# A fused attention and two-layer chain: the first 768 tokens as six tiles of four groups of 32 queries, ordered by a plan that models transfers

## The chip, the cores and the metric

One core of a Trainium2 chip runs the kernel. The metric is device time in microseconds (us) of one execution, less is better. The engines have their usual short names: PE is TensorE (matrix products; PEld its weight loads), DVE is VectorE, ACT is ScalarE, POOL is GpSimd, SP is SyncE, which only issues transfers.

## What is computed

The input is q, k, v (batch 4, 8 heads, 576 tokens, 64 wide) and the weights of two layers. The attention has two parts that are added: a coarse one on means over four tokens, and a local one in which each query sees the keys at a distance under 4.

```python
q_d = q.reshape(B, H, Sd, factor, D).mean(axis=3)    # same for k, v
out_up = np.repeat(sm_attn(q_d, k_d, v_d), factor, axis=2)
mask = np.abs(pos[:, None] - pos[None, :]) < factor
out_local = softmax(where(mask, scale * q @ k.T, -1e9)) @ v
x = (out_up + out_local), tokens as rows             # 2304 x 512
h = x @ w_in;  g = s * relu(h) ** 2 + b;  x = g @ w_out       # 2048 wide
out = ((x @ w_a) * (x @ w_b)) @ w_out2                        # 1536 wide
```

All is float32 to the outside. Inside, each large operand is split into a high and a low part, and a product is the sum of three.

## The kernel before

Every piece of work is a task with an engine, an assumed duration, the tasks it needs, the buffers it takes and gives back, and a due time. `Program.order` plays all tasks through once while the program is built, takes the one that can start first (ties: the one due first), and so writes out the order of every engine. The assumed times set that order alone; on the chip each engine runs its list in order and waits on semaphores.

The work comes in phases. The first layer goes over six blocks of 384 tokens (`BLOCKS`), each with 16 steps of the hidden width (`a_iter`: products `h` at L1059 to L1061, ReLU and square on ACT, split on DVE at L1087, products `acc` at L1102 to L1104, two steps later). The second layer goes over three blocks of 768 tokens. Ahead of block 0 and alongside it, the ramp makes what it needs:

- `down` (from L553): the coarse part, for each batch and each of four pairs of heads. DVE or POOL sums q and k over four tokens (L582; L584 and L585), PE makes the scores (L620), DVE and ACT the softmax (L634 to L662), PE transposes and multiplies by the values (L671, L691), ACT copies to `up` (L703). For batch 0 the values are summed by DVE (L603). For later batches `pool_in` loads them and lets six transfers, issued by POOL, add to them in memory (L551).
- `tile_job` (from L729): the local part of 96 tokens (`TQ`), for tokens 0 to 767. The scores of 96 queries against 102 keys (`TW`) for 8 heads are two products with the mask (L774) and eight with q and k (L780). DVE takes maxima (L802), ACT makes eight exponentials with their sums (L816), DVE normalizes (L824 to L831), PE transposes (L839), ACT copies (L849), PE multiplies by the values (L857), DVE adds the coarse part (L871), and `split_x` makes the high and the low part (L497, L501).
- `w_slice` (from L367): each of 32 weight slices of the first layer comes in a 64-bit form; three ACT instructions (L349, L342, L378) and three of DVE (L354, L362, L383) turn it into the two parts.

For tokens from 768 on, `unit` makes the local part on DVE (L908 to L1015), in the time of the blocks before. The buffers of the ramp are named in `RAMP_BUFS`; `keep_warm` fills waits of PE ahead of the first step with products of zeros (L273).

## Time and profile before

| | us |
|---|---|
| median of 3 runs | 933.05 |
| all runs | 932.78, 933.05, 938.63 |
| profiled execution, span from first to last instruction | 932.3 |
| what lies around it, median less span | 0.75 |
| PE busy in the span | 913.2 (98%) |
| DVE busy | 789.9 (85%) |
| ACT busy | 497.4 (53%) |
| first product `h` of block 0 | 59.2 |

The profiled execution has no time of its own in the results beside its span, so the span is set against the median. A busy share is an average over phases: in the first 150 us DVE and ACT are far above theirs. A row of a timeline gives start and length; the lengths overlap by some 0.1 to 0.2 us, so what an instruction costs its engine is the step from its start to the next start.

### The profile page before, as it was taken

To read this page: it belongs to the slowest core of one execution; us is meant where nothing else is said; L and a number is where in the kernel's file an instruction comes from. 1 tells how busy PE (TensorE), PEld (TensorE's weight loads), DVE (VectorE), ACT (ScalarE), POOL (GpSimd) and SP (SyncE) were. 2 spreads that over 40 slices of the span, in tenths; PEclk is the share of its full clock that TensorE was granted. 3 is DMA by queue.
4 is the path that set the end of the run, shared out by engine and by line. 5 is a ranking of instruction groups with operands and counts; after the bars stand their busy time and mean duration, and the time that the engine had idled before them with its cause. 6 is when DMAs were issued, how large, how long until landed. Compare 5 with 4: busy or idle time off the path is not lost.

```text
span 932.3 us, 14367 instructions
## 1 busy us (share of the span) xinstructions
PE 913.2 (98%) x5319; PEld 847.0 (91%) x5319; DVE 789.9 (85%) x1388; ACT 497.4 (53%) x1144; POOL 69.7 (7%) x70
## 2 busy tenths in 40 slices
PE   8988999999999999999999999999999999999997
PEld 4667989998999899999999999999999999999996
DVE  6988998999999999995977999879877778877753
ACT  4989995345445443535988555335433336433322
POOL 2241201021322200000000000000000000000000
PEclk9998999999999999999999999999999999999999
DMA  7869626224354332313477342012200010300001
GB/s 206 241 174 332 156 90 194 82 82 133 115 115 114 103 107 69 102 29 136 148 262 261 122 122 82 23 44 81 102 22 3 24 43 13 102 29 18 1 1 69
DMA packets 46864, 96.76 MB, mean 104 GB/s; under 512 B 6393, under 2 KB 21337, under 8 KB 46409
## 3 DMA queue, kind: packets, MB, share of 16 engines
q1 hardware_dynamic: 39160, 92.77, 31.0%
q0 software_dynamic: 7200, 2.67, 2.5%
q8 instruction: 42, 0.69, 0.3%
q10 hardware_dynamic: 432, 0.39, 0.1%
q14 instruction: 30, 0.24, 0.1%
HBM read 83.22 MB, written 12.58 MB: 103 GB/s over the span
## 4 chain that ended last, share of the span: by engine, by line
PE 84%; DVE 5%; ACT 4%; issue 3%; DMA 2%; POOL 1%; SPq 0%; ACTq 0%
PE ab L1347 28%; PE acc L1102 7%; PE acc L1103 6%; PE h L1059 6%; PE acc L1104 6%; PE h L1061 6%; PE h L1060 6%; PE acc L1488 5%; PE acc L1489 5%; PE acc L1487 5%; DVE pr L969 1%; DMA pv<-in_vd_dram 1%; ACT z L342 1%; DMA tq<-in_bmask_dram 1%; ACT w L378 1%
## 5 line engine op out<-in xcount | busy, mean ns | idle before, releaser
L1347 PE MATMUL ab<-xo,w 128*128 128x384 f32 x1376 | 273.7, 338 | 0.4 <-DVE u L1390 0.4
L1347 PEld LDWEIGHTS ab<-xo,w 128*128 128x128 f32 x1376 | 246.1, 188 | 16.3 <-DVE u L1390 0.7
L1102 PE MATMUL acc<-gh,w 128*128 128x384 f32 (+1 forms) x384 | 134.2, 350 | 4.0 <-ACT w L816 2.0
L1103 PE MATMUL acc<-gl,w 128*128 128x384 f32 x384 | 131.2, 342 | 0.0
L1059 PE MATMUL h<-xsh,w 128*128 128x384 f32 x384 | 131.1, 341 | 0.0
L1104 PE MATMUL acc<-gh,w 128*128 128x384 f32 (+1 forms) x384 | 130.5, 340 | 0.0
L1061 PE MATMUL h<-xsh,w 128*128 128x384 f32 x384 | 129.0, 336 | 0.0
L1060 PE MATMUL h<-xsl,w 128*128 128x384 f32 x384 | 129.0, 336 | 0.0
L1076 ACT ACTIVATE u<-h 128x384 f32<-128x384 f32 x96 | 47.1, 491 | 116.3 <-PE h L1061 114.9
L1463 ACT ACTIVATE gh<-u 128x384 fp32r<-128x384 f32 x69 | 36.2, 524 | 84.6 <-DVE u L1424 50.5
L1102 PEld LDWEIGHTS acc<-gh,w 128*128 128x128 f32 x384 | 73.0, 190 | 8.1 <-ACT w L816 2.6
L1059 PEld LDWEIGHTS h<-xsh,w 128*128 128x128 f32 x384 | 72.2, 188 | 2.4 <-issue 2.0
L1103 PEld LDWEIGHTS acc<-gl,w 128*128 128x128 f32 x384 | 73.1, 190 | 0.9 <-DVE gl L1087 0.9
L1104 PEld LDWEIGHTS acc<-gh,w 128*128 128x128 f32 x384 | 73.0, 190 | 0.0
L1060 PEld LDWEIGHTS h<-xsl,w 128*128 128x128 f32 x384 | 72.2, 188 | 0.0
L1061 PEld LDWEIGHTS h<-xsh,w 128*128 128x128 f32 x384 | 72.1, 188 | 0.0
L1087 DVE TENSOR_TENSOR gl<-u,gh 128x384 fp32r<-128x384 f32 x96 | 54.3, 565 | 15.4 <-ACT gh L1083 15.2
L1371 ACT ACTIVATE w<-ab 128x384 f32<-128x384 f32 x31 | 15.2, 491 | 95.2 <-PE ab L1347 93.4
L1489 PE MATMUL acc<-w,gl 128*128 128x512 f32 x138 | 54.4, 394 | 0.0
L1488 PE MATMUL acc<-w,gh 128*128 128x512 f32 x138 | 54.3, 394 | 0.0
L1487 PE MATMUL acc<-w,gh 128*128 128x512 f32 x138 | 54.2, 393 | 0.0
L354 DVE TENSOR_SCALAR w<-w 128x512 uint16<-128x512 f32 x61 | 45.6, 767 | 8.3 <-ACT w L349 8.0
(207 smaller groups left out, 1743.9 us busy)
## 6 DMA issues: line engine op xcount, KB each, us to landing
w<-in_w_a_dram SPq DMA_DIRECT2D x26, 512.0 KB
w<-in_w_o_dram SPq DMA_DIRECT2D x25, 512.0 KB
bk<-in_ku_dram SPq DMA_DIRECT2D x22, 320.0 KB
bk<-in_vu_dram SPq DMA_DIRECT2D x22, 320.0 KB
w<-wod SPq DMA_DIRECT2D x12, 512.0 KB
w<-in_w_b_dram SPq DMA_DIRECT2D x10, 512.0 KB
x2d<-ev SPq DMA_DIRECT2D x24, 192.0 KB
x<-x2d SPq DMA_DIRECT2D x3, 1536.0 KB
```

The lines of the kernel that those rows point to most:

```text
L1059: nc.tensor.matmul(out=st["h"], lhsT=w[:, 0, k], rhs=hi[:, k], start=(k == 0), stop=False)
L1060: nc.tensor.matmul(out=st["h"], lhsT=w[:, 0, k], rhs=lo[:, k], start=False, stop=False)
L1061: nc.tensor.matmul(out=st["h"], lhsT=w[:, 1, k], rhs=hi[:, k], start=False, stop=(k == HP - 1))
L1076: A_.activation(out=st["u"], in_=st["h"], func=ACTF.Relu)
L1087: V.tensor_tensor(out=st["lo"], in0=st["u"], in1=st["hi"][:, :n].bitcast(F32), op=ALU.subtract)
L1102: nc.tensor.matmul(out=acc, lhsT=wh, rhs=st["hi"], start=(f == 0), stop=False)
L1103: nc.tensor.matmul(out=acc[:, :n], lhsT=wh, rhs=st["lo"], start=False, stop=False)
L1104: nc.tensor.matmul(out=acc, lhsT=wl, rhs=st["hi"], start=False, stop=(f == FA - 1))
L1347: nc.tensor.matmul(out=o, lhsT=w[:, k], rhs=x, start=(not more and k + n == 0), stop=(k == 1 and n == 2), skip_group_check=more,)
L1487: nc.tensor.matmul(out=acc, lhsT=gh, rhs=w[:, 0], start=first, stop=False)
L1488: nc.tensor.matmul(out=acc, lhsT=gh, rhs=w[:, 1], start=False, stop=False)
L1489: nc.tensor.matmul(out=acc, lhsT=gl, rhs=w[:, 0], start=False, stop=last)
```

## The change

Tokens 0 to 767 are worked on in six tiles of 128 tokens, each of four groups of 32 queries that see 38 keys each (`TQ` 32, `TW` 38, `NQ` 4). The groups lie side by side in the partitions (rows 0, 32, 64, 96) of one score bank, so a row of scores has 8 x 38 = 304 columns instead of 8 x 102 = 816. DVE takes the maxima and subtracts them, writing each head into 64 columns, ACT makes one exponential of the whole tile, DVE sums it. Two heads at a time go through one transposition of 128 x 128 and lie at rows 0 and 64; the values are loaded twice for that, by four transfers a tile (32 and 6 rows at rows 0 and 64). One tile (512 to 639) has tokens of two batches. Scores and outputs are 32 products each instead of 8.

Besides: the values of batch 0 are summed by two additions for each pair of heads, from one load into a `w` buffer. The casts of the mask and of the unit matrix go from DVE to POOL, as does a clearing of the exponentials' two buffers. ACT loads the exponential's table by a small instruction at the start. The summed q and k have four buffers each instead of one, the exponentials two of their own. The plan now models transfers: sixteen engines and partition groups (`Wire`, `wires`), a queue of eight, a transfer's start and landing, and POOL's adding transfers one after another; its due times and assumed times of PE are new.

```diff
-TQ = 96
+TQ = 32
-JOBS = ["TTTTTT", "TTUUU", "UUUUu", "uUUUU"]
+NQ = 4
+TT = NQ * TQ
+JOBS = ["G" * 18, "GGGGGGUUU", "UUUUu", "uUUUU"]
...
-T0, STEP = 40.2, 4.018 / 384
-LEAD = 26.6
-DUE_DOWN = (12.1, 7.8, 2.1, 22.5)
-DUE_NEXT = (60.0, 0.0)
-DUE_TILE = (8.3, 20.6, 22.0)
-DUE_JOB = (11.6, 11.7, 14.9)
...
-WARM, FILL_MIN, FILL_MAX = 18, 1, 20
...
-RAMP_BUFS = {"dq": 2, "dk": 2, "dv": 2, "qd": 1, "kd": 1, "vp": 4, "tq": 1, "tk": 1, "tv": 2, "e": 1, "x": 1, "z": 2}
+T0, STEP = 29.1, 4.018 / 384
+LEAD = 28.4
+DUE_DOWN = (12.1, 3.1, 6.3, 19.4)
+DUE_NEXT = (72.9, 0.0)
+DUE_TILE = (9.3, 25, 22.0)
+DUE_JOB = (11.6, 13.1, 12.9)
...
+WARM, FILL_MIN, FILL_MAX = 18, 0, 20
...
+RAMP_BUFS = {"dq": 2, "dk": 2, "qd": 4, "kd": 4, "tq": 1, "tk": 1, "tv": 1, "e": 2, "x": 1, "z": 2}
...
+            for n, parts in enumerate(t.dma):
+                done = wire.send(s + (DMA_START + ISSUE * n if t.eng == "SP" else POOL_START), parts) + DMA_LAND
+                t.end = max(t.end, done)
+                if t.eng == "SP":
+                    landed.append(done)
+                else:
+                    adding = done + POOL_NEXT
...
+def wires(rows, pieces, size, base=0, adds=False):
+
+    n = max(i for i in range(1, 17) if rows % i == 0)
+    per = rows // n
+    took = per * pieces * (0.038 if adds else 0.003 + size / 21.4e3)
+    engines = [(i, took, {(base + i * per) // 8, (base + i * per + per - 1) // 8}) for i in range(n)]
+    ports = {}
+    for r in range(base, base + rows):
+        ports[r // 8] = ports.get(r // 8, 0.0) + pieces * size * (0.2 if adds else 1.0) / 20e3
+    return engines, list(ports.items())
 
...
+
     def consts():
+        n = n_bufs["r"]["e"]
+        add("POOL", 2.0, e_init, acq=[("re",)] * n, rel=["re"] * n, due=-1e6)
...
+        add(name, cost(3 * TW), mc_fn, ["bm"], ["const"], rel=["rtq"], due=DUE_CONST + 5)
 
...
-                    "POOL" if r else "SP", 1.25, fn, (), [("pv", b)] if r == 3 else (), () if r + kh else [("pv",)], (), due,
-                    [t[kh]] if r else [t[0]] if kh else after, seen=6.0,
+                    "POOL" if r else "SP", 1.25 if r else ISSUE, fn, (), [("pv", b)] if r == 3 else (), () if r + kh else [("pv",)], (), due,
+                    [t[kh]] if r else [t[0]] if kh else after, order=kh if r == 0 else 0, seen=0.1, dma=[wires(HK, HP, 512, 0, r > 0)],
...
-            return st["vp", kh] if b == 0 else pooled[b][:, kh, hp]
+            def lv(p):
...
+
...
+            def vprep(p):
+                x = st["v"]
+                eng.tensor_tensor(out=x[:, :, 0:2], in0=x[:, :, 0:2], in1=x[:, :, 2:4], op=ALU.add)
+                eng.tensor_tensor(out=x[:, :, 0], in0=x[:, :, 0], in1=x[:, :, 1], op=ALU.add)
...
+            st["v"] = tv_slot(p[0])
+            for a, r in parts:
+                for u in range(2):
+                    nc.sync.dma_start(
+                        out=st["v"][u * 64 + a:u * 64 + a + r],
+                        in_=tv[j0:j0 + NQ, a:a + r, u * HP * D:(u + 1) * HP * D].rearrange("g k (h d) -> k g h d", d=D),
+                    )
+
+        parts = ((0, 32), (32, TW - 32))
+        t_v = add(
+            "SP", 4 * ISSUE, l_v, (), [("tv", i)], [("rtv", "w")], after=after, seen=0.1,
+            dma=[wires(r, NQ, 1024, u * 64 + a) for a, r in parts for u in range(2)],
+        )
...
+            sc = st["sc"] = [bank(p[h], [TT, HP, TW], "sc") for h in range(2)]
+            runs = [(0, NQ)] if len(set(variant)) == 1 else [(g, g + 1) for g in range(NQ)]
...
+                for g, e in runs:
+                    nc.tensor.matmul(
+                        out=sc[h][g * TQ:e * TQ], lhsT=identb[:, g:e].rearrange("p g q -> p (g q)"),
+                        rhs=bmaskb[:, variant[g]].unsqueeze(1).to_broadcast([TQ, HP, TW]), start=True, stop=False,
+                    )
...
+                    for g in range(NQ):
+                        q, k, k0, k1 = qk(g, hp)
+                        nc.tensor.matmul(
+                            out=sc[h][g * TQ:g * TQ + TQ, hp, k0:k1], lhsT=q[h * D:h * D + D], rhs=k[h * D:h * D + D],
+                            start=False, stop=(hp == HP - 1),
+                        )
+
...
+            nb = st["nb"] = pools[ph].tile([TT, 2, HP], F32, tag="tnb", name="tnb", bufs=6)
             for h in range(2):
-                V.tensor_reduce(out=nb[:, h * HP:h * HP + HP], in_=st["sc"][h], axis=AX.X, op=ALU.max)
-
-        def m2_fn(p):
-            V.tensor_scalar(out=st["nb"], in0=st["nb"], scalar1=-scale, scalar2=None, op0=ALU.mult)
-
-        chain("DVE", [(2 * dve(HP * TW), m_fn), (0.07, m2_fn)], [("tsc", i)], [("tnb", i)])
+                V.tensor_reduce(out=nb[:, h], in_=st["sc"][h], axis=AX.X, op=ALU.max)
+
+        def d_fn(p):
+            st["w"] = e_slot(ts.picks[2])
+            e = st["w"][:, :NH * 64].rearrange("p (m h u k) -> p h u m k", m=2, h=2, u=2)
+            for h in range(2):
+                V.tensor_tensor(
+                    out=e[:, h, :, :, :TW], in0=st["sc"][h].rearrange("p (u m) k -> p u m k", u=2),
+                    in1=st["nb"][:, h].rearrange("p (u m) -> p u m", u=2).unsqueeze(3).to_broadcast([TT, 2, 2, TW]),
+                    op=ALU.subtract,
+                )
...
+        half = 2 * dve(HP * TW)
+        chain("DVE", [(half, m_fn), (half, d_fn)], [("tsc", i)], [("tnb", i)], [pick(ts, 0), pick(ts, 1)])
...
+            A_.activation(out=e_view(), in_=e_view(), func=ACTF.Exp, scale=scale)
...
+        def n0_fn(p):
+            sm = st["sm"] = pools[ph].tile([TT, NH], F32, tag="tsm", name="tsm", bufs=6)
+            V.tensor_reduce(out=sm, in_=e_view(), axis=AX.X, op=ALU.add)
...
+            e, sm = e_view(), st["sm"]
+            V.tensor_tensor(out=e, in0=e, in1=sm.unsqueeze(2).to_broadcast([TT, NH, TW]), op=ALU.mult)
+
+        chain("DVE", [(dve(NH * TW), n0_fn), (0.07, n1_fn), (0.12, n2_fn), (dve(NH * TW), n3_fn)], [("te", i)], [("ta", i)])
...
-            at = st["at"] = [bank(p[h], [TW, HP, TQ], "at") for h in range(2)]
-            for h in range(2):
-                for hp in range(HP):
-                    nc.tensor.transpose(at[h][:, hp], st["e"][:, h * HP + hp], ident[:TQ, :TQ])
+            at = st["at"] = bank(p[0], [128, HP, TT], "at")
+            for n in range(HP):
+                nc.tensor.transpose(at[:, n], st["w"][:, n * 128:n * 128 + 128], ident)
...
-            aT = st["aT"] = st["w"][:TW, :2 * HP * TQ].rearrange("p (a h q) -> p a h q", a=2, h=HP)
-            for h in range(2):
-                A_.activation(out=aT[:, h], in_=st["at"][h], func=ACTF.Copy)
-
-        add("ACT", 2 * act(HP * TQ, True), c_fn, [("tat", i)], [("taT", i)], rel=[pick(tt, 0), pick(tt, 1)])
+            aT = st["aT"] = st["w"][:, :HP * TT].rearrange("p (a q) -> p a q", a=HP)
+            A_.activation(out=aT[:64 + TW], in_=st["at"][:64 + TW], func=ACTF.Copy)
...
+            o = st["o"] = [bank(p[u], [128, 2, TT], "o") for u in range(2)]
+            for n in range(HP):
+                m, h = divmod(n, 2)
+                for g in range(NQ):
+                    for u in range(2):
+                        nc.tensor.matmul(
+                            out=o[u][h * D:h * D + D, m, g * TQ:g * TQ + TQ], lhsT=st["v"][u * 64:u * 64 + TW, g, n],
+                            rhs=st["aT"][u * 64:u * 64 + TW, n, g * TQ:g * TQ + TQ], start=True, stop=True,
+                        )
```

On DVE, a tile among the first four, before (`tnb`: maxima, `tsm`: sums, `sc`: scores, `vp`: pooled values of batch 0):

```order
L603 TENSOR_REDUCE vp<-dv 72x128 x2
L802 TENSOR_REDUCE tnb<-sc 96x4 x2
L824 TENSOR_SCALAR tsm<-tsm 96x8
L805 TENSOR_SCALAR tnb<-tnb 96x8
L827 RECIPROCAL tsm<-tsm 96x8
L831 TENSOR_TENSOR w<-w,tsm 96x816
```

and now (L732 is of the coarse part):

```order
L732 TENSOR_TENSOR w<-w,sm 72x576
L889 TENSOR_REDUCE tnb<-sc 128x4 x2
L895 TENSOR_TENSOR e<-sc,tnb 128x2x2x38 x2
L911 TENSOR_REDUCE tsm<-e 128x8
L914 TENSOR_SCALAR tsm<-tsm 128x8
L917 RECIPROCAL tsm<-tsm 128x8
L921 TENSOR_TENSOR e<-e,tsm 128x8x38
```

The multiplication of 816 columns becomes one of 304, a subtraction and a sum are new, and the instruction behind the subtraction is the sum, which needs ACT's exponential. The value reductions (L603) are gone.

On POOL, the second batch's preparation (`dk`, `dq` are summed to `kd`, `qd`; the number tells one buffer's use from another's) and the adding transfers (`pv`), before:

```order
L585 TENSOR_TENSOR qd_348<-dq_259 128x144
L551 DMA pv_181<-in_vd_dram 72x4x128 x4
L584 TENSOR_TENSOR dk_343<-dk_343 128x144x2
L585 TENSOR_TENSOR kd_676<-dk_343 128x144
L584 TENSOR_TENSOR dq_377<-dq_377 128x144x2
L585 TENSOR_TENSOR qd_707<-dq_377 128x144
L551 DMA pv_181<-in_vd_dram 72x4x128
L584 TENSOR_TENSOR dk_469<-dk_469 128x144x2
```

and now, from the end of the second pair's preparation on:

```order
L659 TENSOR_TENSOR qd_554<-dq_320 128x144
L625 DMA pv_376<-in_vd_dram 72x4x128
L658 TENSOR_TENSOR dk_548<-dk_548 128x144x2
L659 TENSOR_TENSOR kd_641<-dk_548 128x144
L658 TENSOR_TENSOR dq_550<-dq_550 128x144x2
L659 TENSOR_TENSOR qd_734<-dq_550 128x144
L658 TENSOR_TENSOR dk_618<-dk_618 128x144x2
L659 TENSOR_TENSOR kd_774<-dk_618 128x144
L658 TENSOR_TENSOR dq_630<-dq_630 128x144x2
L659 TENSOR_TENSOR qd_807<-dq_630 128x144
L625 DMA pv_376<-in_vd_dram 72x4x128 x5
L625 DMA pv_1408<-in_vd_dram 72x4x128 x6
```

Before, one add stood ahead of the first preparation, four behind the first pair's and one behind the second pair's. Now one stands behind the second pair's and five behind the last, with the six of the next batch (`pv_1408`) right behind them.

On PE, where the second batch's summed values (`pv`) are first read, before:

```order
L1061 MATMUL h<-xsh,w 128x384
L620 MATMUL sc<-kd,qd 72x144 x4
L671 MATMUL at<-ident,w 72x72 x8
L691 MATMUL o<-w,pv 64x144 x4
L774 LDWEIGHTS identb
L774 MATMUL sc<-bmaskb,identb 96x408
```

and now:

```order
L1197 MATMUL acc_1188<-gh_1303,w_1300 128x386
L1198 MATMUL acc_1188<-gl_1327,w_1300 128x384
L1199 MATMUL acc_1188<-gh_1303,w_1300 128x386
L762 MATMUL o_1361<-w_565,pv_376 64x144 x4
L762 MATMUL o_1369<-w_727,pv_376 64x144 x4
L762 MATMUL o_1378<-w_817,pv_376 64x144 x4
L762 MATMUL o_1389<-w_917,pv_376 64x144 x4
L928 MATMUL at_1402<-ident_75,e_1197 128x128 x4
L1154 MATMUL h_1412<-xsh_119,w_1347 128x384
```

Before, they are read after six `h` products of block 0, for one pair of heads at a time; now all four pairs are read in one piece, after five groups of `h` and four of `acc`.

## Rows read from the trace of the kernel before

**Rows 1.** Busy time by stretch: PE, PEld, DVE, ACT, POOL; granted clock, DMA share, GB/s.
```profile
...
64.40:142.30 77.90, 73.78 (x446) 68.47 (x446) 70.87 (x137) 76.54 (x180) 8.85 (x6) 0.96 0.63 193
147.90:508.80 360.90, 360.48 (x2161) 350.60 (x2161) 326.93 (x483) 194.27 (x435) 39.49 (x38) 1.00 0.41 125
```

**Rows 2.** Single lines over the run: duration min/median/max ns, first and last start.
```profile
...
L1059 PE MATMUL h<-xsh,w x384: 331/336/446, 59.2 to 504.1; 128*128 128x384 f32 x192
...
L383 DVE TENSOR_TENSOR w<-z,w x32: 645/689/744, 51.0 to 142.3; 128x512 fp32r<-128x512 f32 x32
```

**Rows 3.** Timeline of ACT: start, length, instruction (idle before it, releaser).
```profile
...
22.60 0.36 ACT L816 ACTIVATE w<-sc,tnb 96x102 f32<-96x102 f32 x1
22.83 0.22 ACT L816 ACTIVATION_READ_ACCUMULATOR w<-sc,tnb 96x1 f32 x1
...
25.16 0.74 ACT L683 ACTIVATE w<-at 72x288 f32<-72x288 f32 x2
...
30.73 0.87 ACT L849 ACTIVATE w<-at 102x384 f32<-102x384 f32 x2
31.47 0.31 ACT L703 ACTIVATE up<-o 128x144 f32<-128x144 f32 x1
...
60.55 0.68 ACT L349 ACTIVATE w<-w 128x512 int32<-128x512 uint16 x1
61.11 1.25 ACT L342 ACTIVATE z<-w 128x512 f32<-128x512 f32 x2
```

**Rows 4.** Timeline of DVE: a wait at 8 us, and a tile after 32 us.
```profile
...
8.14 0.75 DVE L582 TENSOR_REDUCE kd<-w 128x144 f32<-128x576 f32 x1 [3.10 <-PE sc L620]
...
32.52 1.99 DVE L603 TENSOR_REDUCE vp<-dv 72x128 f32<-72x512 f32 x2
34.42 1.06 DVE L802 TENSOR_REDUCE tnb<-sc 96x4 f32<-96x408 f32 x2
35.40 0.16 DVE L824 TENSOR_SCALAR tsm<-tsm 96x8 f32<-96x8 f32 x1
...
35.83 1.00 DVE L831 TENSOR_TENSOR w<-w,tsm 96x816 f32<-96x816 f32 x1
36.76 1.06 DVE L802 TENSOR_REDUCE tnb<-sc 96x4 f32<-96x408 f32 x2
```

**Rows 5.** Timeline of TensorE: small products of a tile; the end of block 0.
```profile
...
35.59 0.94 PE L780 MATMUL sc<-w 64*96 64x102 f32 x16
...
36.75 0.88 PE L857 MATMUL o<-w,tv 102*64 102x96 f32 x16
...
144.75 0.34 PE L1059 MATMUL h<-xsh,w 128*128 128x384 f32 x1
...
147.90 0.33 PE L1102 MATMUL acc<-gh,w 128*128 128x386 f32 x1
```

**Rows 6.** Timeline of POOL, adding transfers; TensorE, the first product that reads their sum.
```profile
...
42.14 1.19 POOL L551 DMA_DIRECT2D pv<-in_vd_dram  x1 [9.15 <-issue]
...
84.98 1.19 POOL L551 DMA_DIRECT2D pv<-in_vd_dram  x1 [9.81 <-issue]
95.41 1.66 POOL L551 DMA_DIRECT2D pv<-in_vd_dram  x1 [9.24 <-issue]
...
106.25 1.60 POOL L551 DMA_DIRECT2D pv<-in_vd_dram  x1 [3.28 <-issue]
111.39 1.67 POOL L551 DMA_DIRECT2D pv<-in_vd_dram  x1 [3.54 <-issue]
...
61.76 0.71 PE L691 MATMUL o<-w,pv 72*64 72x144 f32 x8
```

**Rows 7.** Timeline of DVE, then of TensorE, at the start of block 2.
```profile
...
216.83 0.68 DVE L501 TENSOR_TENSOR xsl<-x,xsh 128x512 fp32r<-128x512 f32 x1
...
218.23 0.44 PE L1059 MATMUL h<-xsh,w 128*128 128x384 f32 x1
```

More of the change, by code (lines that the diff above doesn't have):

```diff
@@ L84 @@
         "eng", "dur", "fn", "deps", "succ", "acq", "picks", "rel", "due", "lead", "share", "num", "left", "ready", "start",
-        "end", "fill", "seen",
+        "end", "fill", "seen", "dma", "order", "wait",
     )
@@ L278, in fn @@
             nc.sync.dma_start(out=dst, in_=src)
[L280 removed]
+        dma = [wires(rows, pieces, nbytes / rows / pieces, base)]
+        return add("SP", ISSUE, fn, reads, writes, acq, rel, due, after, seen=0.1, dma=dma)
     WIDE = ("att", "h", "acc")
@@ L342, in z_fn @@
             A_.activation(out=st["z"], in_=high, func=ACTF.Copy, scale=2.0 ** -112)
-        tz = add("ACT", 0.56, z_fn, [("st", k)], [("z", k)], acq, after=first)
+        tz = add("ACT", 0.56, z_fn, [("st", k)], [("z", k)], acq, after=first, wait=PATIENCE)
         def a_fn(picks):
```

310 lines of the change are left out of this document (160 added, 150 removed).

## The prediction

> **What bounds the kernel now.** I read the busy time by stretch first [rows 1]. From 147.9 us on, TensorE is busy without a gap (360.48 of 360.90 us) and its work there is untouched by the change. What can move lies before. That ramp has three marks [rows 2]: the first product of block 0 (L1059) at 59.2, the first weight slice finished by DVE (L383) at 51.0, the 32nd and last at 142.3. The last accumulation of block 0 starts at 147.9 [rows 5]; call this mark M. The kernel's end follows M as long as nothing after it runs dry. At TensorE's own pace of 0.175 us a product (18 products from 144.75 to 147.90 [rows 5]) the 384 products ahead of M take 67.2 us; they took 88.7. The reason: between 64.4 and 142.3 ACT is busy 76.54 of 77.90 us and DVE 70.87 [rows 1]. ACT makes the weight slices, three instructions for each, and between them runs the tiles' exponentials. So the ramp is ACT's, with DVE a few us behind it.
>
> **Change part by part.** I price by the step from one instruction's start to the next one's.
>
> ACT: eight exponentials of a tile run from 22.60 to 25.16, 2.56 us, and its two copies from 30.73 to 31.47, 0.74 [rows 3]. Eight tiles: 26.4 us go. What comes are six exponentials of 304 columns and six copies of 512. Neither shape is in the trace: bounds are 0.23 (a 102-column exponential, 22.60 to its read at 22.83) and 0.56 (512 columns, 60.55 to 61.11) [rows 3]; I take 0.35 and 0.50, 5.1 us. ACT saves 21 us (20 to 24). The table load is moved to where ACT is idle anyway.
>
> DVE: two maxima over 408 columns take 0.98 (34.42 to 35.40), the three small steps 0.43, the multiplication over 816 columns 0.93, a value reduction 0.95 [rows 4]. Eight tiles and eight reductions: 18.7 + 7.6 = 26.3 us, and 0.5 for the two casts that go to POOL. 408 and 816 columns give 1.1 ns a column and 0.05 fixed. So a new tile costs two maxima and two subtractions of 152 columns (0.21 each), a sum and a multiplication of 304 (0.38 each) and two small steps (0.27): 1.9 us, six times 11.3; the value sums become four pairs of additions, 512 and 256 columns, 0.60 + 0.33, 3.7. The adding of the coarse half and the split have as many elements as before. DVE saves about 12 us (9 to 14, if the new shapes cost nothing more or each costs a third more).
>
> The head, up to the first slice on DVE at 51.0: in DVE's order the old head holds six tiles' maxima and multiplications and all eight reductions (21.6 us), the new one four tiles, the additions, and 4.2 us of the second batch's coarse softmax and 1.1 of weight work that now stand ahead: 16.7. Net 4.5 us less, with the smaller steps. The 3.10 us that DVE waited for TensorE at 8.14 [rows 4], because the buffer for the pooled keys was single, goes too: there are four now, and next late is the data itself. Against it, a tile now waits between the subtraction and the sum for ACT's one exponential, with little behind it in DVE's order: I charge 0.65 for each of four. First slice: 51.0 - 4.5 - 3.1 + 2.6 = 46. The first product stands behind the scores of all of batch 1, which need POOL's preparation, but that is earlier in POOL's order now; I put it at 47 (42 to 53) instead of 59.2.
>
> From there to M: TensorE has 67.2 us of products, plus one tile's scores, two tiles' transposes and outputs, and the coarse outputs of batch 1. A tile's score products are 64 records instead of 16, the outputs 64 instead of 16, of 38 and 32 columns instead of 102 and 96. Old: 16 records in 0.94 and 0.88 us [rows 5], 0.055 each. If time goes with columns, an output is 1.2 us; if with records, 3.5. I take 2.0 for either, as the masks come on top 2.5 for the scores. A tile's transposes I take at 0.55, batch 1's coarse outputs at 0.65 each as before (0.71 with its tail [rows 6]): 2.5 + 1.1 + 4.0 + 2.6 = 10.2. That makes 77.4. Summing the new orders from first to last slice, DVE needs 71 us and ACT 73. All three lie within 7 us, so none is bound alone: I add 2.
>
> Trainium skill, "TensorEngine Tiling (Array Packing)", section on instruction overhead: a product of few columns takes as long as one of 60, so a tiling factor should not be taken from a dimension that is already small. By it an output would be an estimated 64 x 0.055 x 60/96 = 2.2 us, which the old rows, all of 96 columns and more, can't confirm; the sum would be 0.5 us longer.
>
> The chained adds: POOL adds batch 1's values in six transfers that each wait for the one before. Before, five of the six go out by 42.14 and TensorE reads them from 61.76 on [rows 6]. Now one goes out ahead of the last preparations and five behind them, and TensorE's order has batch 1's outputs (L762) behind five products and four accumulations, 19 us of work, about 21 us after its first: at 68. The step from add to add was 10.43 (84.98 to 95.41) with weights crowding the queues, 5.14 (106.25 to 111.39) with few [rows 6]. The second add I put at 33, an estimate: two preparations, the first add and two more preparations go ahead of it, and the old fifth went out at 42. With the middle step, 7.8, the last lands at 33 + 5 x 7.8 = 72. TensorE waits 4 us, and behind it wait ACT's copies L774 in its order, with the weight slices, and one SP load of values with them. Part is caught up since ACT and DVE worked ahead: 2.5. Ends: 0 and 18.
>
> Trainium skill, "DMA: Bandwidth & Descriptors", section on the anatomy of one GpSimd DMA: 2.0 us plus bytes over 436 GB/s for each. For 147 KB that is an estimated 2.3 us, and this wait would be nothing. The trace disagrees: no step from add to add is under 5 us, so it stays in.
>
> M = 47 + 77.4 + 2 + 2.5 = 129 against 147.9: 19 us earlier. Behind M nothing changes: same units, same loads. But DVE is just in time there: the split of block 2's last unit starts at 216.83, its first product at 218.23 [rows 7]. So the end moves by the smaller of the two shifts, M's 19 and that of DVE's last slice, 142.3 - (46 + 71 + some 5 of waits) = 20. The profiled execution's span is 932.3, the median of the runs 933.05, 0.75 around it. 932.3 - 19 + 0.75 = 914.
>
> **Rivals.**
> A. As summed: 914, own range 908 to 920.
> B. The adds decide. With 10.4 us a step the last lands at 85, TensorE stands 17 us, and 4 are left: 929. For: the weight loads are let go just then. Against: the short step of 5.14. If POOL starts five later and a step is 12 to 13 us, the last lands at 98 to 103; from 89 on the gain is gone, and at 101 the time is 945, slower. That is the case on the other side.
> C. Small products go by records: a tile's scores and outputs 3.5 us each, on the path of the first three tiles, and 4 us more behind the first product. First product at 52, M at 138: 923. For: half of what the old products did is loading weights. Against: between them TensorE has warm-up products to drop.
> D. Fewer waits than charged: first product at 42, no wait on the adds, 78 to M at 120: 905. For: ACT's 21 us are on the path nearly in full.
> E. The gain doesn't reach the end, since the units behind M run dry: DVE, held behind TensorE's wait for the adds in its own order, finishes its slices only 5 us earlier, and block 2 waits for it [rows 7]: 928. Against: DVE's sum is 12 us smaller.
>
> **Chances.** A 0.52, D 0.17, C 0.13, B in part (921 to 929) 0.06, B slower 0.04, E 0.08. What a measurement of this kernel tells from no change is about 1%, 9.3 us. Faster by more: A, D, nearly all of C and B in part, 0.86. Within 1%: most of E and what is left of C and B, 0.09. Slower: 0.05. The range runs from D's 905, less 1, to the far side of C, 925.
>
> **What would show it.** Right: the first L1154 near 47, the last L457 near 122, the last accumulation of block 0 near 129, and 932.3 less that shift at the end; ACT below 85% in 64 to 120 with DVE above it. The adds are seen in POOL's steps and in TensorE's wait before L762; the small products in L862 and L947, start to start. Wrong: a first product after 53, a wait over 8 us at L762, or an end that moved less than M.

## The result and the profile after

The two kernels were run in turn: before 935.69 us (median of 4 runs, 932.78 to 938.63), changed 923.4 us (median of 4, 919.97 to 927.55). The ratio is 0.988 with a 95% interval of 0.985 to 0.992, so the change makes the kernel 1.2% faster; by the ratio that is 11.1 us of 935.69, by the two medians 12.3. Forecast were 914, 19 us less than the 933.05 of the runs known then, with a range of 904 to 925: the direction and the range held, the gain is some 60% of what was forecast. The profiled execution took 923.98 us, with a span of 922.2, 10.1 below the span of before.

| mark, us | before | forecast | after |
|---|---|---|---|
| first slice done by DVE | 51.0 | 46 | 51.8 |
| first product of block 0 | 59.2 | 47 | 54.9 |
| last slice done by DVE | 142.3 | 122 | 129.0 |
| last accumulation of block 0 (M) | 147.9 | 129 | 134.6 |
| span | 932.3 | 913.3 | 922.2 |

The marks are read where [rows 2] were, in the view of single lines of the changed kernel (first and last start). L1154 is a product of a block, first at 54.9:

```profile
...
L1154 PE MATMUL h<-xsh,w x384: 331/336/688, 54.9 to 491.0; 128*128 128x384 f32 x192
```

In the same view L457, DVE's last step for a weight slice, from 51.8 to 129.0:

```profile
...
L457 DVE TENSOR_TENSOR w<-z,w x32: 669/690/797, 51.8 to 129.0; 128x512 fp32r<-128x512 f32 x32
```

The changed kernel's busy time by stretch answers to [rows 1] (columns as there). The fourth stretch shows what was forecast, TensorE without a gap. The first shows what was not: for 21 us the granted clock was 0.51, that is, almost wholly the lower level of 1.2 GHz, with TensorE busy all the time, DVE only 61% and ACT 43%. In that stretch of the head (the time up to the first product of block 0) TensorE was the bound. Not all that it did was needed work: 11 of its products in these 21 us, 4.35 us of its busy time, are warm-up products (L328), put ahead of waits that the plan foresaw. The last row goes against the prediction: in 64 to 120 us ACT is busy 55.45 of 56.00 us and DVE 54.29.

```profile
...
22.00:43.00 21.00, 21.00 (x395) 14.88 (x394) 12.80 (x45) 8.95 (x30) 8.67 (x14) 0.51 1.00 268
43.20:54.90 11.70, 10.10 (x253) 7.79 (x250) 10.79 (x28) 9.95 (x31) 3.58 (x3) 0.91 0.52 112
54.90:134.60 79.70, 78.14 (x618) 75.44 (x619) 72.16 (x148) 73.72 (x149) 9.40 (x7) 0.97 0.68 213
134.60:495.70 361.10, 360.27 (x2163) 350.60 (x2162) 328.18 (x486) 195.52 (x439) 44.47 (x38) 1.00 0.41 127
...
64.00:120.00 56.00, 55.02 (x443) 53.08 (x442) 54.29 (x113) 55.45 (x114) 7.60 (x6) 1.00 0.71 225
```

The changed kernel's timeline of TensorE shows the start of it and the prices of the small products. It stood 0.77 us for DVE's L732, up to 21.41; from 22 to 43 the clock was low. At 53.91 it had stood 1.54 us for nothing that the profile names (`issue`). A tile's 64 output records (L947) took 2.37 us there (28.14 to 30.51) and 1.38 at full clock (46.56 to 47.94); a mask 0.30 (51.05 to 51.35) and the 64 score records 0.70 (51.35 to 52.05). The coarse outputs L762 of the second batch came at 79.17, without a wait.

```profile
...
21.41 0.69 PE L741 MATMUL at<-ident,w 72*72 72x72 f32 x8 [0.77 <-DVE w L732]
...
28.14 2.44 PE L947 MATMUL o<-e,tv 38*64 38x32 f32 x64
30.51 0.52 PE L328 MATMUL pw<-wz 128*128 128x408 bf16 x1
...
46.56 1.46 PE L947 MATMUL o<-e,w 38*64 38x32 f32 x64
47.94 0.69 PE L741 MATMUL at<-ident,w 72*72 72x72 f32 x8
...
51.05 0.37 PE L854 MATMUL sc<-bmaskb,identb 32*32 32x152 bf16 x8
51.35 0.77 PE L862 MATMUL sc<-tk,tq 64*32 64x38 f32 x64
52.05 0.32 PE L741 MATMUL at<-ident,w 72*72 72x72 f32 x2
53.91 0.94 PE L741 MATMUL at<-ident,w 72*72 72x72 f32 x6 [1.54 <-issue]
...
79.17 2.34 PE L762 MATMUL o<-w,pv 72*64 72x144 f32 x32
```

Its timeline of DVE in the same head. L675, L676 and L732 are one pattern, run four times: 0.66, 0.42 and 0.75 us in the third, 1.06, 0.56 and 1.21 in the fourth, when POOL's first preparation had begun (18.03, below). L732 is what TensorE waited for. Further down DVE waits for TensorE (2.79 at 28.24, and seven more such waits, 7.5 us in all from 24 to 43).

```profile
...
16.70 0.66 DVE L675 TENSOR_TENSOR w<-w 72x512 f32<-72x512 f32 x1
17.39 0.42 DVE L676 TENSOR_TENSOR w<-w 72x256 f32<-72x256 f32 x1
...
17.80 0.75 DVE L732 TENSOR_TENSOR w<-w,sm 72x576 f32<-72x576 f32 x1
...
18.56 1.06 DVE L675 TENSOR_TENSOR w<-w 72x512 f32<-72x512 f32 x1
19.66 0.56 DVE L676 TENSOR_TENSOR w<-w 72x256 f32<-72x256 f32 x1
20.15 1.21 DVE L732 TENSOR_TENSOR w<-w,sm 72x576 f32<-72x576 f32 x1
...
28.24 0.82 DVE L704 TENSOR_REDUCE nb<-sc 72x2 f32<-72x288 f32 x2 [2.79 <-PE sc L690]
```

The new shapes cost what was taken (start to start): the multiplication 0.39, ACT's one exponential 0.36, and in a later stretch of DVE's timeline two maxima 0.46 (38.95 to 39.41) and two subtractions 0.40:

```profile
...
38.95 0.54 DVE L889 TENSOR_REDUCE tnb<-sc 128x4 f32<-128x152 f32 x2 [0.79 <-PE sc L862]
39.41 0.15 DVE L725 TENSOR_SCALAR sm<-sm 72x4 f32<-72x4 f32 x1
...
39.59 0.48 DVE L895 TENSOR_TENSOR e<-sc,tnb 128x152 f32<-128x152 f32 x2
39.99 0.16 DVE L728 RECIPROCAL sm<-sm 72x4 f32<-72x4 f32 x1
```

The changed kernel's timeline of POOL, which answers to [rows 6]: the first preparation at 18.03, the second add at 35.08, the sixth at 63.39. Steps from add to add are 8.20, 4.91, 4.46 and 10.74; the packets of the sixth end at 74.25.

```profile
...
18.03 1.05 POOL L658 TENSOR_TENSOR dk<-dk 128x288 f32<-128x288 f32 x1 [7.53 <-DMA dk<-in_kT_dram]
...
35.08 1.21 POOL L625 DMA_DIRECT2D pv<-in_vd_dram  x1
43.28 1.19 POOL L625 DMA_DIRECT2D pv<-in_vd_dram  x1 [6.99 <-issue]
48.19 1.20 POOL L625 DMA_DIRECT2D pv<-in_vd_dram  x1 [3.72 <-issue]
52.65 1.19 POOL L625 DMA_DIRECT2D pv<-in_vd_dram  x1 [3.27 <-issue]
63.39 1.52 POOL L625 DMA_DIRECT2D pv<-in_vd_dram  x1 [9.55 <-issue]
```

At the start of the second layer 3 us of the lead are lost. TensorE waits 1.81 us at 506.18 for a product of DVE (L1507), and the clock is 0.67 from 505 to 510; before, the longest such wait was 0.36. TensorE's timeline there:

```profile
...
506.18 1.83 PE L1443 MATMUL ab<-xo,w 128*128 128x384 f32 x6 [1.81 <-DVE w L1507]
```

DVE's timeline has two instructions of 0.95 and 1.22 us ahead of that L1507:

```profile
...
502.91 0.95 DVE L1305 TENSOR_TENSOR x<-x 128x768 f32<-128x768 f32 x1
503.78 1.22 DVE L1389 TENSOR_TENSOR w<-w 128x1024 fp32r<-128x1024 f32 x1
...
505.58 0.55 DVE L1507 TENSOR_TENSOR w<-w,ab 128x384 f32<-128x384 f32 x1
```

### The profile page after: what moved, and what is told of

Same layout as the page of the kernel before. It is cut to its first block, busy times and chain, and to the rows that moved or that the text cites. A ratio compares the mean times of both kernels' runs of the same rounds, so it can differ in the third digit from the quotient of the medians.

```text
span 922.2 us, 15173 instructions
## 1 busy us (share of the span) xinstructions
PE 909.3 (99%) x5794; PEld 848.4 (92%) x5794; DVE 777.4 (84%) x1390; ACT 476.2 (52%) x1011; POOL 71.8 (8%) x74
## 4 chain that ended last, share of the span: by engine, by line
PE 90%; DVE 6%; ACT 2%; issue 1%; DVEq 0%; ACTq 0%
PE ab L1443 29%; PE h L1154 7%; PE acc L1197 7%; PE h L1155 6%; PE h L1156 6%; PE acc L1198 6%; PE acc L1199 6%; PE acc L1584 5%; PE acc L1585 5%; PE acc L1583 5%; PE pw L328 1%; PE o L762 1%; PE sc L690 1%; PE o L947 1%; PE at L741 1%
## 5 line engine op out<-in xcount | busy, mean ns | idle before, releaser
L1443 PE MATMUL ab<-xo,w 128*128 128x384 f32 x1312 | 267.7, 338 | 1.8 <-DVE w L1507 1.8
L1443 PEld LDWEIGHTS ab<-xo,w 128*128 128x128 f32 x1312 | 235.2, 188 | 16.9 <-DVE w L1507 2.1
L1197 PE MATMUL acc<-gh,w 128*128 128x384 f32 (+1 forms) x384 | 132.1, 344 | 1.5 <-DVE gh L1184 0.9
L1154 PE MATMUL h<-xsh,w 128*128 128x384 f32 x384 | 132.0, 344 | 0.1
L1199 PE MATMUL acc<-gh,w 128*128 128x384 f32 (+1 forms) x384 | 129.5, 337 | 0.0
L1559 ACT ACTIVATE gh<-u 128x384 fp32r<-128x384 f32 x68 | 35.7, 524 | 87.3 <-DVE u L1520 50.4
L1154 PEld LDWEIGHTS h<-xsh,w 128*128 128x128 f32 x384 | 72.8, 190 | 2.2 <-issue 1.8
L1467 ACT ACTIVATE w<-ab 128x384 f32<-128x384 f32 x34 | 16.7, 491 | 100.6 <-PE ab L1443 100.5
L1182 DVE TENSOR_TENSOR gl<-u,gh 128x384 fp32r<-128x384 f32 x96 | 53.6, 558 | 13.7 <-ACT gh L1178 13.3
L1175 ACT ACTIVATE u<-u 128x384 f32<-128x384 f32 x96 | 50.5, 526 | 2.0
L1178 ACT ACTIVATE gh<-u 128x384 fp32r<-128x384 f32 x96 | 50.5, 526 | 1.8
L1443 PE MATMUL ab<-xo,wx 128*128 128x384 f32 x200 | 50.0, 345 | 0.0
L1064 DVE TENSOR_TENSOR pr<-s,bk 128x1792 f32<-128x1792 f32 (+1 forms) x26 | 49.2, 1893 | 0.7
```

Source lines behind the costliest of these rows:

```text
L1064: V.tensor_tensor(out=pr, in0=st["s"][:, h].unsqueeze(3).to_broadcast([128, R, 7, D]), in1=window(st["v", h], R), op=ALU.mult,)
L1154: nc.tensor.matmul(out=st["h"], lhsT=w[:, 0, k], rhs=hi[:, k], start=(k == 0), stop=False)
L1175: A_.activation(out=st["u"], in_=st["u"], func=ACTF.Square)
L1178: A_.activation(out=st["hi"][:, :n], in_=st["u"], func=ACTF.Copy)
L1182: V.tensor_tensor(out=st["lo"], in0=st["u"], in1=st["hi"][:, :n].bitcast(F32), op=ALU.subtract)
L1197: nc.tensor.matmul(out=acc, lhsT=wh, rhs=st["hi"], start=(f == 0), stop=False)
```

## The experiments

**The clock.** The plan before put at least one warm-up product ahead of each of TensorE's tasks in the ramp (`FILL_MIN` 1), the changed one only where it foresees a wait. `e1_one_filler` puts one back everywhere, and `e2_before_no_forced` takes the unneeded ones out of the kernel before, each with all other work in the same order.

```diff
-            keep_warm(t.fill)
+            keep_warm(max(t.fill, t.warm))     # e1: t.warm is 1 up to the first accumulation
-            keep_warm(t.fill)
+            keep_warm(t.fill - t.warm)         # e2, in the kernel before: without the forced ones
```

> The changed kernel with at least one warm-up product ahead of every task of TensorE before the first accumulation, order of all other work unchanged. Theory (the clock): in the profile of the changed kernel TensorE's granted clock is 0.50 from about 22.9 to 43.2 us, and the first L1154 comes at 54.9, because the small products stand there nearly without warm-up products. Then here the clock is 1.00 between 20 and 45, the first L1154 starts at 47 to 49, the last accumulation of block 0 at 127 to 130, and the time is 915 to 919, 4 to 8 us under the changed kernel. Rival (order): the head is late because of waits between DVE and ACT, and the clock costs nothing; then the first L1154 stays at 54 or later, since some 35 warm-up products of 0.17 us come on top, and the time is 923 to 926.

> The kernel before, without those warm-up products that were put ahead of a task although its plan saw no wait there; order otherwise unchanged. Theory (the clock): the granted clock, 1.00 from 0 to 50 before, falls to 0.50 somewhere between 15 and 50, the first L1059 comes at 62 to 68 instead of 59.2, and the time is 936 to 942. Rival (order): the clock stays or its fall costs nothing, TensorE has 46 rows less, the first L1059 comes at 57 to 59.5 and the time is 930 to 934.

`e1_one_filler`: 924.06 us (923.74 to 925.16), ratio to before 0.990 (0.988 to 0.992): no better than the changed kernel. Its first L1154 came at 55.2 and M at 134.1, and the time as the rival had it, yet the mechanism of the theory is half there. The clock held to 34 us, then fell after TensorE had stood 1.47 us in the middle of a group. Its busy time by stretch, with the granted clock third from the end:

```profile
...
20.00:34.00 14.00, 12.71 (x345) 8.88 (x328) 11.79 (x36) 6.69 (x22) 8.95 (x13) 1.00 0.92 212
34.20:45.00 10.80, 8.79 (x151) 5.71 (x152) 5.02 (x19) 2.87 (x11) 3.34 (x5) 0.53 1.05 295
```

And the row of TensorE's timeline where it stood:

```profile
...
34.24 1.63 PE L947 MATMUL o<-e,w 38*64 38x32 f32 x56 [1.47 <-issue]
```

`e2_before_no_forced`: 935.47 us, ratio 1.002 (1.000 to 1.003). The clock fell, to a mean of 0.66 from 20 to 45 us where it had been 1.00, and the first product hardly moved: first L1059 at 59.4 against 59.2, near the rival's 57 to 59.5, with a time between the two expectations. On the way it did cost something: the kernel before has DVE busy 24.33 of these 25 us, e2 20.99, and DVE's first slice (L383) came at 54.7 instead of 51.0. Busy time of the kernel before in that stretch:

```profile
...
20.00:45.00 25.00, 22.55 (x252) 15.02 (x253) 24.33 (x53) 23.03 (x116) 5.94 (x6) 1.00 0.86 231
```

And of e2:

```profile
...
20.00:45.00 25.00, 22.67 (x194) 16.30 (x196) 20.99 (x46) 21.10 (x107) 4.90 (x5) 0.66 0.83 218
```

What took up most of the 3.7 us shows in the timeline of TensorE in the kernel before: ahead of the first product it waited 2.55 us for POOL's preparation, and e2 doesn't wait for POOL there.

```profile
...
54.69 1.24 PE L620 MATMUL sc<-kd,qd 64*72 64x144 f32 x8 [2.55 <-POOL qd L585]
```

So without the forced products the lower clock went with a later slice in the kernel before too, but the wait for POOL hid most of it from the first product; in the changed kernel no such wait stands there. Warm-up products alone don't keep the clock.

**Two parts undone.** `e3_one_buffer` gives the summed q and k one buffer each again, `e4_old_dues` takes the due times of before. Both are planned anew.

```diff
-"qd": 4, "kd": 4
+"qd": 1, "kd": 1                              # e3
-T0, STEP = 29.1, 4.018 / 384
+T0, STEP = 40.2, 4.018 / 384                  # e4, with LEAD and the four DUE_ lines of before
```

> The changed kernel with one buffer each for the summed q and k instead of four (order planned anew). By the prediction the single buffer costs DVE 3.1 us in the head: first slice L457 some 3 us later than 51.8, time 925 to 928. Rival: DVE waits for TensorE and transfers there anyway, and the time is 921 to 925.

> The changed kernel with the due times of before (start, lead, coarse part, next batch, tiles, units). If the gain comes from the work that the new tiles save on ACT and DVE, most of it stays: 921 to 927. If it comes from the new due times, it is lost: 930 to 938, with the first L1154 at 58 or later.

`e3_one_buffer`: 932.41 us (ratio 0.999, 0.997 to 1.000), worse than either theory said. The prediction's 3.1 us for the buffers isn't what is seen: the first slice came at 46.1, earlier than 51.8, and M at 142.3. The new plan put other work first, TensorE stood 3.77 and 2.19 us, the second time for an adding transfer, and the clock was 0.71 to 0.80 from 60 to 80. What four buffers save by themselves stays open.

`e4_old_dues`: 931.27 us (ratio 0.996, 0.993 to 0.999), but in two heaps: 925.13 to 926.75 (4 runs), where most of the gain stays, and 930.83 to 935.41 (6 runs), where it is lost. The one profile is of the slower heap, with the first L1154 at 58.0; what it shows may be what parts them, a profile of the quicker heap is missing. TensorE stood 3.23 and 1.53 us in the head with no engine named, and in its timeline L762 stands 3.62 us for an adding transfer:

```profile
...
83.19 1.82 PE L762 MATMUL o<-w,pv 72*64 72x144 f32 x20 [3.62 <-DMA pv<-in_vd_dram]
```

POOL's timeline of the same run has that transfer, the sixth, going out only at 79.17:

```profile
...
79.17 1.20 POOL L625 DMA_DIRECT2D pv<-in_vd_dram  x1 [6.32 <-issue]
```

After that wait TensorE's clock was 0.74 from 80 to 100. This is the mechanism of rival B. Both runs say that the new tiles alone don't hold the gain: with the old due times, or with one buffer, most of it or all went. No run has the old tiles with the new plan, so how much of the gain is the tiles' and how much the plan's stays open.

**Transfers and the order at the second layer.** `e5_filler_late_w` and `e6_late_w` issue the first four weight loads behind the third tile's loads, with and without the extra warm-up products. `e7_switch` moves four of DVE's instructions behind the third L1507 of the second layer; its ramp is the changed kernel's, instruction for instruction.

```diff
-        for t, picks in P.order():
+        plan = P.order()
+        late = [x for x in plan if x[0].num in MOVED]      # e5, e6: the loads 131, 138, 145, 152; e7: 2490, 2128, 2130, 2147
+        plan = [x for x in plan if x not in late]
+        at = 1 + [x[0].num for x in plan].index(BEHIND)    # e5, e6: 441; e7: 2073
+        plan[at:at] = late
+        for t, picks in plan:
```

> The kernel e1_one_filler with its first four weight loads issued behind the third tile's loads. In e1_one_filler TensorE stood 1.47 us at 32.77 in the middle of a group of L947, while a 16 KB packet of instructions was under way from 31.55 to 32.95 (the transfers' share was 1.09), then its clock was 0.50 to 45 us and the first L1154 came at 55.2 all the same. Theory (clock and code): with fewer transfers around 32 us the packet comes in time, the clock stays at 1.00 to 45, the first L1154 starts at 48 to 50, and the time is 916 to 920. Rival (the chain through DVE and ACT sets the head): first L1154 at 54 or later and 922 to 925.

> The changed kernel, without added warm-up products, with its first four weight loads issued behind the third tile's loads. Theory (clock): the clock falls near 22 us as in the changed kernel, the first L1154 stays at 54 to 56, time 922 to 925. Rival (transfers alone hold the head): the preparations on POOL (L658, waits of 2.48, 1.29 and 0.47 us for their loads) come earlier, the first L1154 at 50 to 52 and the time 918 to 921.

> The changed kernel with four instructions of DVE (second L1305, L1389, L1399, one L1367) put behind the third L1507 at the start of the second layer. In the changed kernel TensorE waits 1.81 us there at 506.18 for that L1507, and its clock is 0.67 in 505 to 510; the lead over the kernel before shrinks from 13.1 us (last accumulation of block 5) to 10.1 at the end. Theory (order at the switch): the wait goes, the clock stays, 920 to 921.5. Rival (something else ends last there, the load of x or a weight): the wait moves to the next product, 923 to 924.

`e5_filler_late_w`: 922.43 us (0.987, 0.983 to 0.990); first L1154 at 52.4, M at 137.1. `e6_late_w`: 924.68 (0.990, 0.986 to 0.994); 55.9 and 134.9. `e7_switch`: 923.58 (0.988, 0.985 to 0.991); 51.0 and 135.7. None differs from the changed kernel. For e6 and e7 that is as the theory and the rival, in this order, had it, though e6's clock was low only from 24 to 34 and its late head came with two stops without a named engine, 1.15 and 3.04 us; in e5 the head came earlier, between the two expectations, without bringing the time down. At the second layer the wait only moved: e7 has 1.17 and 1.29 us there for ACT's L1467 and DVE's L1473.

The find is in e7's ramp, the same program as the changed kernel's, 4 us quicker in its head and 1 us later at M. A profile is one execution, so heads of two profiles that lie closer than these 4 us tell little apart. Its timeline of TensorE:

```profile
...
21.72 0.70 PE L741 MATMUL at<-ident,w 72*72 72x72 f32 x8 [0.22 <-DVE w L732]
...
38.06 0.47 PE L690 MATMUL sc<-kd,qd 64*72 64x144 f32 x3 [2.75 <-issue]
...
51.01 0.44 PE L1154 MATMUL h<-xsh,w 128*128 128x384 f32 x1 [0.62 <-ACT w L753]
...
78.41 3.63 PE L762 MATMUL o<-w,pv 72*64 72x144 f32 x28 [3.68 <-DMA pv<-in_vd_dram]
```

TensorE waited only 0.22 us for L732 (0.77 in the changed kernel's profile), the clock was 1.00 to 38 us, the first product came at 51.0. Then it stood 3.68 us for the sixth add, whose packets ended at 78.04, and the clock was 0.85 from 70 to 80. In e5 it stood 3.50 us, for packets that ended at 79.29. As these profiles read, the head and the adds are two bounds of nearly the same height, and either hides the other.

**The adds.** `e8_adds_early` spreads the adds over POOL's preparations, `e9_adds_early_filler` has e1's warm-up products as well, `e10_one_add` leaves five of the six adds out.

```diff
 # e8, e9: moved in the way of e7's edit (not with it), the adds 357, 358, 359 behind the preparations 366, 381, 396
-        for t, picks in P.order():
+        for t, picks in (x for x in P.order() if x[0].num not in range(358, 363)):   # e10
```

> The changed kernel with POOL's second batch of adding transfers spread: one add behind each of the first three pairs' preparations and three behind the last (before this edit one behind the second pair and five behind the last). In the changed kernel the sixth add's packets end at 74.25 and TensorE reads the sum at 79.17 without waiting; in e7_switch and e5_filler_late_w, whose first L1154 came at 51.0 and 52.4, they end at 78.04 and 79.29 and TensorE waits 3.68 and 3.50 us, and block 0 ends at 135.7 and 137.1. Theory (the adds are the next bound behind the head): the sixth add ends by 68, TensorE never waits at L762, and where the head is quick (first L1154 at 51) block 0 ends at 131, where it is slow (55) at 134; over the runs 919 to 922. Rival (POOL's waits between the adds delay the preparations, and with them the scores L690 of the last pairs): first L1154 at 56 or later and 925 to 929.

> e8_adds_early with at least one warm-up product ahead of every task of TensorE before the first accumulation. Theory (clock and adds each hide the other): both bounds are gone, first L1154 at 50 to 53, no wait at L762, block 0 ends at 130 to 132 and the time is 916 to 920. Rival (the warm-up products cost as much as the clock): same as e8_adds_early within 2 us.

> The changed kernel without five of the second batch's six adding transfers: its pooled values are sums over two instead of four tokens for one half and one token for the other. It prices the chain of adds, POOL's preparations unchanged. Theory: with a head as in the changed kernel (first L1154 at 54 to 55) no more than 1 us is gained at the end of block 0, with a quick one (51) 4 to 5 us; over the runs 919 to 921. Rival (the adds cost nothing): 923 to 924 as the changed kernel.

`e10_one_add`: 919.7 us, ratio 0.984 (0.981 to 0.987), in the theory's 919 to 921 and some 4 us better than the changed kernel, though the intervals still touch; with five adds left out it doesn't do all the work. Its profile has a quick head and no wait at L762, and block 0 ends at 130.0, within 1 us of the forecast's 129. TensorE's timeline of e10:

```profile
...
50.79 0.44 PE L1154 MATMUL h<-xsh,w 128*128 128x384 f32 x1 [0.29 <-ACT w L753]
...
74.73 0.47 PE L762 MATMUL o<-w,pv 72*64 72x144 f32 x4
```

`e8_adds_early`: 923.96 us (0.988, 0.985 to 0.990). The sixth add's packets end at 68.6, about as expected (by 68), but this profile's head is slow (55.2), so L762 comes at 78.87 and nothing is gained: M 134.1. The time over all runs missed the theory's 919 to 922. `e9_adds_early_filler`: 925.08 (0.990, 0.987 to 0.993). TensorE stood 1.35 and 1.55 us in the head for nothing that another engine did, the clock fell twice, and the first L1154 came at 60.2. The theory failed; the time is the rival's, within 2 us of e8, and the head is later than either had it.

**A version with both bounds moved.** `e11_outputs_late` puts L762 and what hangs on it six product groups later. `e12_pool_late` is the same and holds POOL's first preparation back until DVE's last L732 of the head is done.

```diff
 # e11, e12: moved in the way of e7's edit (not with it), L762 and its copies, two tiles' outputs and the next value loads behind the product group 1042
+ # e12, ahead of POOL's first preparation
+ G.tensor_tensor(out=warm[:HK, 1:2], in0=late, in1=late, op=ALU.add)    # late: a column that L732 wrote
```

> The changed kernel with the second batch's coarse outputs (L762), their copies, the two tile outputs that need them and the next batch's value loads moved behind six more groups of TensorE's block 0 products (6.3 us of plan). Theory (where the head is quick, the last adding transfer is the bound at L762): TensorE never waits at L762, since the products read the sum some 6 us later; with a head as in e7_switch (first L1154 at 51) block 0 ends at 130 to 132 instead of 135.7, with one as in the changed kernel's trace (55) at 134; over the runs 919 to 921. Rival (TensorE runs dry of weight slices in place of it): the wait moves to L1154 or L1197 at 75 to 85 us, same or larger, and the time is 923 to 926.

> e11_outputs_late, and on POOL a one-column addition ahead of its first preparation that reads what DVE's last softmax product of batch 0 (L732) wrote, so that POOL starts behind it. In the traces of the changed kernel and of e8_adds_early POOL starts at 18.0 and 19.0 us, DVE's L675 and L676 beside it take 1.06 and 0.56 us instead of 0.66 and 0.42, TensorE waits 0.77 and 0.73 us for L732, its clock is 0.50 for the next 20 us and the first L1154 comes at 54.9 and 55.2; in e7_switch and e10_one_add POOL starts at 20.2 and 20.0, TensorE waits 0.2 to 0.3, and it comes at 51.0 and 50.8. Theory (that start decides the head): TensorE waits under 0.3 us there, the clock is 1.00 from 20 to 33, first L1154 at 50 to 52, block 0 ends at 129 to 131, 917 to 919.5. Rival (chance or transfers decide): the clock falls before 30 as often, first L1154 at 53 to 56, time as e11_outputs_late or above.

`e11_outputs_late`: 927.63 us (0.993, 0.990 to 0.995), rather slower than the changed kernel, if not by more than the intervals. The add is waited for no more, but two tiles' outputs, their additions and splits now stand in one piece: from 80 to 100 us DVE and ACT are busy 14.7 and 14.5 of 20 us (19.8 both in e8, 19.5 and 19.7 in e10), and block 0 ends at 139.4. The rival, that another wait takes its place, holds in kind; the waits stand elsewhere (0.91 us at 79.47 for DVE, 0.70 at 88.80 for ACT, 0.82 at 91.71), and the time is above its 923 to 926. `e12_pool_late`: 925.59 (0.991, 0.989 to 0.994), also not better than the changed kernel, for the same piece: block 0 ends at 136.4 and the theory's time of 917 to 919.5 is missed. But its head is as the theory had it. Its busy time in the head:

```profile
...
20.00:45.00 25.00, 22.69 (x608) 17.00 (x600) 23.05 (x73) 17.10 (x60) 12.07 (x19) 1.00 0.95 251
```

The same run's timeline of POOL, with the wait for L732 that was put in and the preparation behind it:

```profile
...
21.96 0.19 POOL L654 TENSOR_TENSOR warm<-w 72x1 f32<-72x1 f32 x1 [9.53 <-DVE w L732]
22.11 0.66 POOL L658 TENSOR_TENSOR dk<-dk 128x288 f32<-128x288 f32 x1
```

And its timeline of TensorE, where two groups of small products are cut by stops:

```profile
...
45.55 1.60 PE L947 MATMUL o<-e,w 38*64 38x32 f32 x52 [1.94 <-issue]
...
50.85 0.94 PE L741 MATMUL at<-ident,w 72*72 72x72 f32 x6 [1.63 <-issue]
```

POOL starts at 22.11, DVE's last L732 takes 0.75 us, TensorE doesn't wait for it, the clock stays at 1.00 for the 25 us to 45, and the first slice leaves DVE at 45.5: the forecast's 46. Against e11, which lacks only the addition that holds POOL back and whose clock was low from 24 to 44 us, the slice comes 7.3 us earlier (45.5 against 52.8), the first product 2.8 (51.9 against 54.7). What stands between the slice and that product are two stops of 1.94 and 1.63 us for which the profile names no engine. Each ends 1.4 to 1.5 us after a 16 KB packet of the queue of kind "instruction" has landed (44.0 and 49.5). The DMA queues of e12 from 42 to 46 us (packets, MB, share) have the first of them:

```profile
...
q8 instruction: 1, 0.02, 2.1%
```

So it is in all the traces with the small products: 53.91 and 52.5 in the changed kernel, 34.24 and 32.9 in e1, 38.06 and 36.6 in e7. The reading that fits is that TensorE waits for its own code. Full transfer engines aren't needed for it: their share was 1.12, 1.06 and 1.03 at the first stop of e12 and those of e1 and e7, but 0.34 at the second stop of e12 (48.5 to 51), 0.30 at the 3.04 us of e6 and 0.22 at the stop of the changed kernel:

```profile
...
51.50:54.00 2.50, 0.96 (x67) 0.75 (x57) 2.50 (x6) 1.76 (x4) 1.19 (x1) 0.75 0.22 44
```

The number of packets goes with the number of TensorE's records. The kernel before has 943 products and weight loads up to 60 us, loads four such packets and never stops for one; the changed one has 1747 and loads seven, some 240 to 250 records a packet in both. No run changed the number of records alone, so this cause is argued and not shown.

Side by side, for the profiles of one ramp order (e10 without five adds, e11 with another order behind 75 us):

| run | POOL starts | TensorE waits for L732 | clock low before 50 us | first L1154 | sixth add ends | wait at L762 | M |
|---|---|---|---|---|---|---|---|
| changed | 18.03 | 0.77 | 22 to 43 | 54.9 | 74.3 | 0 | 134.6 |
| e8 | 19.04 | 0.73 | 24 to 44 | 55.2 | 68.6 | 0 | 134.1 |
| e7 | 20.22 | 0.22 | 40 to 43 | 51.0 | 78.0 | 3.68 | 135.7 |
| e10 | 19.95 | 0.33 | 34 to 37 | 50.8 | none | 0 | 130.0 |
| e11 | 19.23 | 0.77 | 24 to 44 | 54.7 | 77.5 | 0 (read later) | 139.4 |

The three with the long wait for L732 are those in which POOL started ahead of DVE's fourth L675 (by 0.2 to 0.5 us); in e7 and e10 it started 0.5 to 0.8 us behind. No version with all the work in it is better than the changed kernel beyond the intervals.

## Why the prediction was right, and where its size was off

**What was right.** ACT saves 21.2 us over the run (497.4 to 476.2; forecast 21), DVE 12.5 (789.9 to 777.4; forecast 12). From the first product to M it took 79.7 us, forecast 82. M is followed by the rest nearly one to one: 13.3 us at M, 13.1 at the last accumulation of block 5 (508.8 to 495.7). The sixth add lands at 74, forecast 72. That the cut in ACT's and DVE's work is what makes the gain is argued from these sums and not isolated by a run, as said at e4.

**The step that failed: the head.** "First slice: 51.0 - 4.5 - 3.1 + 2.6 = 46" gave 46 and measured 51.8, and the first product 54.9 instead of 47, 7.9 us. The sum priced DVE alone, with 0.65 us a tile for waits on ACT. It had no line for TensorE, which before the change ran at full clock there with DVE busy 24.33 of 25 us. With DVE and ACT shorter, TensorE's products in their order are the chain from 22 to 43 us, at half the clock, and the stop of 1.54 us with no engine named comes on top before the first product. DVE waited 7.5 us for TensorE and 1.3 for ACT instead of 2.6. In e12, where TensorE's clock stays up, the first slice comes at 45.5, with 0.8 us of waits for TensorE and 0.7 for ACT: DVE's sum comes out where TensorE doesn't hold it up.

**The adds** were charged 2.5 us and cost nothing in the profiled execution, because TensorE came to L762 at 79.2 and not at 68: the late head, 7.9 of these 11.2 us, paid for them. From the second add (35.08) to the end of the sixth (74.25) the five steps averaged 7.8 us, as charged. "No step from add to add is under 5 us" was misread: POOL's timeline of before has one of 4.80 (101.45 to 106.25 [rows 6]), and the changed kernel one of 4.46; both are far from the 2.3 that they were held against.

```profile
...
101.45 1.52 POOL L551 DMA_DIRECT2D pv<-in_vd_dram  x1 [4.38 <-issue]
```

With a quick head they cost 3.5 to 3.7 us of waiting and a lower clock behind it (e5, e7). Rival B's mechanism is there, and without five of the adds (e10) the time falls by some 4 us. That e10 and the forecast agree at M (130.0 and 129) is chance in part: the small products were cheaper than charged and its head later than 47.

**Small products.** 4.5 us were charged for a tile's scores with masks and outputs; they cost 1.0 and 1.38, 2.4 in all. An output record of 32 columns takes 0.022 us (1.38 / 64), one of 96 took 0.055 [rows 5]: nearly with columns. A score record of 38 columns takes 0.011 (0.70 / 64), half of that; why, no run shows. Rival C, with 0.055 for each, falls. By the Trainium skill, "TensorEngine Tiling (Array Packing)", section on instruction overhead, an estimated 2.2 us was due for the outputs; the trace disagrees, 1.38 at full clock. What was not priced is the other cost that many instructions seem to have, their loading.

**The sign that ACT should show.** "ACT below 85% in 64 to 120 with DVE above it" didn't come: ACT was busy 99% there and DVE 97%. The sign didn't fit the prediction's own sum either, which gave ACT 73 us of some 76 from the first slice to the last; with less other work both engines make the slices sooner and stay as full.

**Behind M.** "Behind M nothing changes" holds up to block 5, then 3.0 us go at the start of the second layer (13.1 to 10.1). e1 and e10 lose 3 to 4 us from M to the end; e7 shows that the wait moves when its DVE work is moved. What ends last there wasn't settled.

The sum: 19 forecast, less 5.6 at M (7.9 in the head, 2.3 back on the way), less 3.2 from M to the end: 10.2, measured 10.1 in the span. The condition for being wrong, "a first product after 53", was met, and the end did move by less than M.

## What to carry to other kernels

When a change takes work off the engine that is the bound, write the sum for the next engine as well, at both levels of TensorE's clock: its waits and its clock cost little at the end while another engine is waited for (e2), and much when none is. Two bounds of nearly equal height hide each other: an experiment that lifts one shows nothing, and the runs split into heaps; leave the suspected work out (as e10) rather than move it. Many small products were cheap by the column here; watch instead for stops that end just behind an instruction packet.
